# Per-expert tile counts read one expert ahead, and a later place for the next expert's first transposes, in a fused attention and mixture-of-experts kernel

## The chip, the cores and the metric

The kernel runs on one core of a Trainium2 chip. The metric is device microseconds of one execution; the number given for the kernel before is the median of three runs. Beside these runs there is one profiled execution, and every duration below comes from it.

## The reference

The reference chains three blocks on 4608 tokens of width 512. The first is attention over keys and values that are mean-pooled by eight. The second sends each token that passes a skip score through one of eight experts, the third is a dense layer with a SoLU and a layer norm. Only the second one matters for the change:

```python
    do_compute = skip_score > 0
    ...
    e_idx = np.argmax(logits, axis=1)
    ...
    for e in range(E):
        mask = e_idx == e
        if not mask.any():
            continue
        h = np.maximum(xc[mask] @ w1[e], 0.0)
        y[mask] = gate_w[mask, None] * (h @ w2[e])
    out[do_compute] = xc + y
```

How many tokens an expert gets is known only at run time.

## The kernel before

The kernel is one instruction stream per engine, in the order in which the Python code is written. It has three stages: attention with routing (about 0 to 228 us), the experts (228 to 620 us) and the dense layer (620 us to the end).

**Routing** scatters each token's index and gate weight into a table, sorted by expert, in HBM. At the end of the attention stage the token counts of the eight experts are turned, on VectorE (DVE), into a small integer tile `nti` in SBUF (lines 785 to 793). A count is in half tiles of 64 tokens, at least 2. `nti` holds four groups of eight: the count, its half (whole tiles of 128), its odd bit, and the half limited to the last table column.

**The expert stage** is a Python loop over e (line 1084). Tokens of one expert are worked off in tiles of 128 by `body(e, q_, work)` (line 965): a gather of the token rows (`gather`, an indirect DMA issued by GpSimd, POOL), four transposes on TensorE (PE) into the one PSUM tile `pxt` with a scaled copy to f16 on ScalarE (ACT, line 922) and the rounding rest on DVE (line 923) (`trans`), four groups of matmuls with the first weight (`mm1_group`, line 938, 24 matmuls a group) each followed by the ReLU on ACT (line 942) and its rounding rest on DVE (line 943), the matmuls with the second weight in two halves (`mm2`, line 950), and `fin`: gate and residual on DVE (line 954) and a scatter by POOL (line 955). Every operand is held as an f16 high part and an f16 rest.

**What lies between the groups** is handed to `body` as a list `work`, one entry after each group, one between the halves of `mm2`, what is left at the end. For the first tile of an expert the list holds the preparation of expert e+1: eight weight pieces (`wnext`, piece i: `w_split` makes the high part on ACT, line 114, and the rest on DVE, line 119; for piece 4 on POOL, lines 116 and 117; then the load of piece i of expert e+2 is queued) and the transposes of the first tile of expert e+1. In the kernel before these transposes are third in the list for every expert, so they stand behind group 2 (counted from 0) and before group 3.

**Half tiles.** An expert with an odd count has one tile of 64 rows more. Its rows' addresses and gates are copied by DVE into `hidx` and `hgat` from a table column that is known only at run time (lines 1010 and 1011), its rows are gathered at the start of the expert (line 1012), and `half(e)` runs under `tc.If(odd[e] > 0)` (line 1114) between the first and the second tile. Its ReLU rest is line 1037, its second matmul line 1041. The second and later tiles stand in nested Ifs on the count (line 1129).

**Counts into registers.** Behind the first tile of expert 0 every engine reads eight counts and eight odd bits from `nti` into registers, and DVE eight column numbers besides (lines 1100 to 1104). An If that isn't taken still keeps order: an engine whose next work needs buffers that the If's body might have used waits until the others have passed it.

In this input expert 0 has an even count (three tiles), experts 1 and 7 are even, expert 4 has one tile, and experts 2, 3, 5 and 6 have a half tile.

Of the kernel before, what the change touches and what calls it, by code (L numbers as in the profile page):

```python
# [10 lines left out]
I32 = mybir.dt.int32  # L11
AF = mybir.ActivationFunctionType
ALU = mybir.AluOpType
# [28 lines left out]
def fused_kernel(  # L42
# [15 lines left out]
    nc = tc.nc  # L58
    V, S, G, T = nc.vector, nc.scalar, nc.gpsimd, nc.tensor
    B, H, SEQ, D = q.shape  # L60
    NTOK, DM = out.shape
    E, _, DF = w1.shape
    NT = NTOK // P
# [9 lines left out]
    cp = ctx.enter_context(tc.tile_pool(name="cp", bufs=1))  # L73
# [47 lines left out]

    tabv = cp.tile([P, NT, 2], F32, name="tabv")
    row = cp.tile([P, NT], I32, name="row")
    nti = cp.tile([1, 4 * E], I32, name="nti")
    tbe = cp.tile([P, E * NT, 2], F32, name="tbe")
    tbs = []
    idx0 = cp.tile([P, 1], I32, name="idx0")
# [2 lines left out]
    with ExitStack() as actx:  # L130
# [653 lines left out]
        cnt = ac.tile([P, E], F32, name="cnt")  # L784
        V.tensor_tensor(cnt, base[rt["n"] % 2][:, 0:E], base0[:, 0:E], ALU.subtract)
        cni = ac.tile([P, E], I32, name="cni")

        V.tensor_scalar(cni, cnt, 63.0, None, ALU.add)
        V.tensor_scalar(cni, cni, 6, None, ALU.logical_shift_right)
        V.tensor_scalar(nti[:, 0:E], cni[0:1, :], 2.0, None, ALU.max)  # L790
        V.tensor_scalar(nti[:, E:2 * E], nti[:, 0:E], 1, None, ALU.logical_shift_right)
        V.tensor_scalar(nti[:, 2 * E:3 * E], nti[:, 0:E], 1, None, ALU.bitwise_and)
        V.tensor_scalar(nti[:, 3 * E:], nti[:, E:2 * E], NT - 1.0, None, ALU.min)
        for i in range(4, 7):
            w_split(0, i)

# [11 lines left out]
    def d_load(i, eng=nc.sync):  # L808
        a = w_in if i < 4 else w_out
        if wide:  # L810
            a = a.bitcast(I32)
        st_ = dst[i % 2]
        if i < 4:
            eng.dma_start(st_, a[i * P:(i + 1) * P, :])
        else:
            j = 2 * (i - 4)
            eng.dma_start(st_.rearrange("p (c d) -> p c d", c=2),
                              a[j * P:(j + 2) * P, :].rearrange("(c p) d -> p c d", p=P))
# [44 lines left out]
    def m_load(i):  # L863
        t_ = xg[gset(E, i)] if i < NPRE else fp.tile([P, DM], F32, tag="x2", name="x2", bufs=3)
        (G if i < NPRE else nc.sync).dma_start(t_, m_rows(xres[P:XROWS, :], i))
        sx[i] = {"x": t_}
# [11 lines left out]
    with ExitStack() as mctx:  # L878
# [5 lines left out]
        tbi = mp_.tile([P, E * NT + 1], I32, name="tbi")  # L884
        tb = tbe
# [16 lines left out]
        hidx = [mp_.tile([P, 1], I32, name=f"hidx{i}") for i in range(2)]  # L902
        hgat = [mp_.tile([P, 1], F32, name=f"hgat{i}") for i in range(2)]

        def gset(e, q_):
            return q_ % 3 if q_ > 2 else 4 + 2 * q_ + e % 2 if q_ else 3 + e % 3

        def tset(e, q_):
                return q_ % 2 if q_ else 2 + e % 2
# [5 lines left out]
        def trans(g_, s_, pe=False, w=P):  # L915
            h_, l_ = xt[s_][:, 0:NKC, 0:w], xt[s_][:, NKC:, 0:w]
            if pe:
                for kc in range(NKC):
                    T.transpose(pxt[:, kc * P:kc * P + w], xg[g_][0:w, kc * P:(kc + 1) * P],
                                ident[0:w, 0:w])  # L920
                px = pxt.rearrange("p (c t) -> p c t", c=NKC)[:, :, 0:w]
                S.activation(h_, px, AF.Copy, scale=SX1)
                V.scalar_tensor_tensor(l_, px, SX1, h_, ALU.mult, ALU.subtract)
                return
            hl = xhl[s_ // 2]
            S.activation(hl[:, 0:DM], xg[g_], AF.Copy, scale=SX1)
            V.scalar_tensor_tensor(hl[:, DM:], xg[g_], SX1, hl[:, 0:DM], ALU.mult, ALU.subtract)
            nc.sync.dma_start_transpose(xt[s_], hl)
# [36 lines left out]
        def body(e, q_, work):  # L965

            c = e * NT + q_
            s_, hb = tset(e, q_), q_ % 2
            if q_ + 2 < nstatic and (q_ or e == 0):
                gather(gset(e, q_ + 2), idx_of(c + 2))  # L970
            if q_ == 0 and e:
                half_rows(e)
            if q_ == 0 and e + 1 < E:
                for j, r in ((e + 2, 0), (e + 1, 1), (e + 1, 2)):
                    if j < E:
                        gather(gset(j, r), idx_of(j * NT + r))

            first = e == 0 and q_ == 0
            pe = q_ < 2
            if q_ + 1 < nstatic and not pe:  # L980
                trans(gset(e, q_ + 1), tset(e, q_ + 1))
            work = list(work)

            def step(n=1):
                for _ in range(n):
                    if work:
                        work.pop(0)()

            for gq in range(4):
                mm1_group(e, s_, hb, gq, q_)  # L990
                if gq == 1 and pe and not first:
                    trans(gset(e, q_ + 1), tset(e, q_ + 1), True)
                step()
            mm2(e, hb, 0, 4)
            if first:
                trans(gset(e, q_ + 1), tset(e, q_ + 1), True)
            elif q_ == 0:
                half_trans()
            step(1)
            mm2(e, hb, 4, 8)  # L1000
            step(len(work))
            fin(gset(e, q_), hb, gate_of(c), idx_of(c))

        HG, HT = 1, 0

        def half_rows(e):
            o_ = hq[e] + e * NT
            V.tensor_scalar(hidx[e % 2], tbi[:, bass.ds(o_, 1)], 0.0, None, ALU.add)  # L1010
            V.tensor_scalar(hgat[e % 2], tb[:, bass.ds(o_, 1), 1], 0.0, None, ALU.add)
            G.indirect_dma_start(out=xg[HG][0:64], out_offset=None, in_=xbuf,
                                 in_offset=bass.IndirectOffsetOnAxis(ap=hidx[e % 2][0:64], axis=0))

# [59 lines left out]
        def wnext(e, i):  # L1074

            w_split(e + 1, i, i == 4)
            if e == 0 and i < 4:
                w_load(e + 1, i + 4, nc.scalar)
            if e + 2 < E:
                w_load(e + 2, i)  # L1080
# [3 lines left out]
        for e in range(E):  # L1084


            last = e + 1 == E
            works = {q_: [] for q_ in range(nstatic)}
            if not last:
                sp = [lambda e=e, i=i: wnext(e, i) for i in range(8)]  # L1090
                works[0] += sp[0:2] + [lambda e=e: trans(gset(e + 1, 0), tset(e + 1, 0), True)] + sp[2:6]
                works[1] += sp[6:]
            if e < 2:
                works[1].append(lambda e=e: d_load(e))
            for n, j in enumerate(DP.get(e, ())):
                works[n if last else n + 1] += [lambda f_=f_, j=j: f_(j)
                                                for f_ in (d_decode, d_split, d_next)]
            body(e, 0, works[0])
            if e == 0:
                cnts = [nc.values_load(nti[0:1, j:j + 1], min_val=2, max_val=2 * NT) for j in range(E)]  # L1100
                hq = [nc.values_load(nti[0:1, 3 * E + j:3 * E + j + 1],
                                     engines=[mybir.EngineType.DVE], min_val=0, max_val=NT - 1) for j in range(E)]
                odd = [nc.values_load(nti[0:1, 2 * E + j:2 * E + j + 1], min_val=0, max_val=1)
                       for j in range(E)]
            if last:
                m_load(0)
                works[1].append(lambda: m_xt(0))
                for i in range(1, NPRE):
                    works[min(i + 1, nstatic - 1)] += (
                        [lambda i=i: m_load(i)] + 3 * [lambda: None] + [lambda i=i: m_xt(i)])  # L1110

            with tc.If(odd[e] > 0):  # L1114
                if e == 0:
                    half_rows(e)
                    half_trans()
                half(e)

            def rest(q_):  # L1120

                if q_ == nstatic:
                    with tc.If(cnts[e] > 2 * q_ + 1):  # L1123
                        n = nc.values_load(nti[0:1, E + e:E + e + 1], min_val=0, max_val=NT)
                        with tc.For_i(nstatic, n, 1, name=f"rest{e}") as j:
                            loop_tile(e, j)
                    return
                todo = [f_ for r in range(q_, nstatic) for f_ in works[r]]
                with tc.If(cnts[e] > 2 * q_ + 1) as full:  # L1129
                    body(e, q_, works[q_])  # L1130
                    rest(q_ + 1)
                if todo:
                    with full.Else():
                        for f_ in todo:
                            f_()

            rest(1)
# [140 lines left out]
```

## Time and profile before

| what | us |
|---|---|
| median of three runs (lowest, highest) | 1006.11 (1002.54, 1011.88) |
| the profiled execution | 1002.64 |
| its span, first to last instruction | 1000.9 |
| PE busy in the span | 889.9 |

The profiled execution is near the lowest of the three runs and 3.47 us below their median; 1.74 us of it lie outside the span. In the rows, times are microseconds from the span's start: start, busy time, engine, line and operation, result and operands, how often, and in brackets the idle time of the engine before it with what ended it. "DVEq L1114" means that the engine was released when DVE's instruction queue passed line 1114. "PEld" is PE's weight load.

### The profile page before, as it was taken

To read this page: it belongs to the slowest core of one execution; us is meant where nothing else is said; L and a number is where in the kernel's file an instruction comes from. 1 tells how busy PE (TensorE), PEld (TensorE's weight loads), DVE (VectorE), ACT (ScalarE), POOL (GpSimd) and SP (SyncE) were. 2 spreads that over 40 slices of the span, in tenths; PEclk is the share of its full clock that TensorE was granted. 3 is DMA by queue.
4 is the path that set the end of the run, shared out by engine and by line. 5 is a ranking of instruction groups with operands and counts; after the bars stand their busy time and mean duration, and the time that the engine had idled before them with its cause. 6 is when DMAs were issued, how large, how long until landed. Compare 5 with 4: busy or idle time off the path is not lost. (4 is left out here: it accounts for less than half of the span.)

```text
span 1000.9 us, 20355 instructions
## 1 busy us (share of the span) xinstructions
PE 889.9 (89%) x7838; PEld 565.3 (56%) x7838; DVE 628.3 (63%) x1419; ACT 430.4 (43%) x1002; POOL 299.3 (30%) x255
## 2 busy tenths in 40 slices
PE   5898899855497888689898999989999999999998
PEld 4687777645375566566676676434444444444443
DVE  7599888996344554665564732666666666666652
ACT  3476667733223343432432321445445344443432
POOL 3692967675213433452331220000000000000000
PEclk9698989987798999899999999999999999999999
DMA  9799867366547555765162641457756656657443
GB/s 284 234 322 330 281 225 253 123 222 191 174 148 241 173 179 160 237 187 178 50 164 80 150 85 55 92 112 135 153 130 138 138 125 124 140 110 149 100 91 88
DMA packets 189310, 163.99 MB, mean 164 GB/s; under 512 B 137296, under 2 KB 145488, under 8 KB 188656
## 3 DMA queue, kind: packets, MB, share of 16 engines
q1 hardware_dynamic: 180880, 140.50, 52.4%
q0 software_dynamic: 7200, 19.57, 6.2%
q10 hardware_dynamic: 1088, 2.10, 0.6%
q8 instruction: 80, 1.31, 0.6%
q14 instruction: 62, 0.51, 0.2%
HBM read 94.95 MB, written 38.01 MB: 133 GB/s over the span
## 5 line engine op out<-in xcount | busy, mean ns | idle before, releaser
L1215 PE MATMUL po<-woh,zt 128*128 128x512 f16 x576 | 176.7, 379 | 3.1 <-ACT o L1218 2.0
L1152 PE MATMUL ph<-wih,xt 128*128 128x512 f16 x576 | 176.7, 379 | 1.0 <-DVEq L1123 1.0
L1215 PEld LDWEIGHTS <-zt 128*128 128x128 f16 x864 | 84.4, 98 | 105.7 <-issue 2.3
L1152 PEld LDWEIGHTS <-xt 128*128 128x128 f16 x864 | 84.4, 98 | 103.2 <-issue 1.5
L1191 POOL TENSOR_TENSOR rr<-va,mhalf 128x1 f32<-128x1 f32 x36 | 19.8, 549 | 342.9 <-DVE va L1190 342.9
L1174 ACT ACTIVATE wst<-ph,ng 128x512 f32<-128x512 f32 x72 | 48.8, 682 | 158.2 <-DVE ng L1170 146.0
L942 ACT ACTIVATE hh<-ph 128x256 f16<-128x256 f32 x104 | 39.0, 380 | 172.5 <-PE ph L938 164.3
L1152 PE MATMUL ph<-wil,xt 128*128 128x512 f16 x288 | 109.2, 379 | 0.0
L1215 PE MATMUL po<-wol,zt 128*128 128x512 f16 x288 | 109.2, 379 | 0.0
L938 PE MATMUL ph<-xt,wsb 128*128 128x128 f16 x1536 | 95.4, 225 | 13.7 <-PEq L1129 9.2
L938 PEld LDWEIGHTS <-wsb 128*128 128x128 f16 x1536 | 92.6, 101 | 19.2 <-issue 16.5
L943 DVE SCALAR_TENSOR_TENSOR hl<-ph,hh 128x256 f16<-128x256 f32 x104 | 43.0, 421 | 60.8 <-ACT hh L942 59.1
L938 PE MATMUL ph<-xt,wsa 128*128 128x128 f16 x960 | 60.7, 225 | 22.3 <-DVEq L1114 13.7
L950 PE MATMUL py<-wsb,hh 128*128 128x512 f16 x256 | 76.2, 379 | 0.0
L938 PEld LDWEIGHTS <-wsa 128*128 128x128 f16 x960 | 58.4, 102 | 26.3 <-DVEq L1114 14.2
L1206 DVE SCALAR_TENSOR_TENSOR zl<-wst,zh 128x1024 f16<-128x1024 f32 x36 | 44.1, 1225 | 45.3 <-ACT zh L1204 45.3
L955 POOL DMA_INDIRECT xres<-yo,tbi x26 | 28.8, 1109 | 140.0 <-DVE yo L954 77.2
L1178 DVE SCALAR_TENSOR_TENSOR wst<-ph,wst 128x512 f32<-128x512 f32 x72 | 49.0, 692 | 30.5 <-ACT wst L1174 30.5
L505 PE MATMUL px<-vbh,ah 128*128 128x148 f16 (+1 forms) x320 | 52.7, 231 | 15.4 <-DVE lraw L538 11.6
L269 POOL TENSOR_TENSOR kv<-kv 128x1280 f32<-128x1280 f32 (+3 forms) x28 | 57.1, 2041 | 22.2 <-DMA kv<-in_k_dram 21.0
L1157 DVE TENSOR_REDUCE mx<-ph 128x1 f32<-128x512 f32 x72 | 49.4, 686 | 21.1 <-PE ph L1152 21.1
L950 PEld LDWEIGHTS <-hh 128*128 128x128 f16 x416 | 39.0, 98 | 41.1
(384 smaller groups left out, 1841.0 us busy)
## 6 DMA issues: line engine op xcount, KB each, us to landing
wst<-in_moe_w_dram SPq DMA_DIRECT2D x60, 512.0 KB, 4.7
out_dram<-o SPq DMA_DIRECT2D x36, 256.0 KB, 2.4
x<-xres SPq DMA_DIRECT2D x33, 256.0 KB, 3.3
kv<-in_v_dram SPq DMA_DIRECT2D x8, 1024.0 KB, 9.7
xbuf<-xs SPq DMA_DIRECT2D x16, 512.0 KB, 3.5
xres<-xs SPq DMA_DIRECT2D x16, 512.0 KB, 7.8
kv<-in_k_dram SPq DMA_DIRECT2D x7, 1024.0 KB, 8.8
qm<-in_q_dram SPq DMA_DIRECT2D x7, 1024.0 KB, 9.1
```

Source lines behind the costliest of these rows:

```text
L269: eng.tensor_tensor(x_[:, :, 0:r, :], x_[:, :, 0:r, :], x_[:, :, r:2 * r, :], ALU.add)
L505: T.matmul(hd[sl, a, h:h + x1 - x0, :], s_, w_[rw, c0 + x0:c0 + x1, :], start=(n == 0 and bl == 2 * a), stop=(n == 2 and bl == 2 * a + 2))
L938: T.matmul(o_, ww[:, kc * DF + fc * P:kc * DF + (fc + 1) * P], xt[s_][:, x0 + kc, :], start=(n == 0), stop=(n == 11))
L942: S.activation(hh[hb][:, sl], ph, AF.Relu)
L943: V.scalar_tensor_tensor(hl[hb][:, sl], ph, 0.0, hh[hb][:, sl], ALU.max, ALU.subtract)
L950: T.matmul(py[hb], xx[:, fc * P:(fc + 1) * P], ww[:, fc * DM:(fc + 1) * DM], start=(fc == 0 and n == 0), stop=(fc == NFC - 1 and n == 2))
L1152: T.matmul(ph, xt[:, xx, :], ww[:, ws], start=(n == 0), stop=(n == 11))
L1157: V.tensor_reduce(sx[i]["mx"][:, half:half + 1], ph, axis=AX.X, op=ALU.max)
L1174: S.activation(e_[:, o_], ph[a], AF.Exp, bias=ng, scale=CE, accum_out=s2[:, a:a + 1])
L1178: V.scalar_tensor_tensor(u_[:, o_], ph[a], 1.0, e_[:, o_], ALU.mult, ALU.mult, accum_out=su[:, a:a + 1])
L1206: V.scalar_tensor_tensor(zl, u_, SZ, zh, ALU.mult, ALU.subtract)
L1215: T.matmul(po, zt[:, xx, :], ww[:, ws], start=(fc == 0 and n == 0), stop=(fc == NFC - 1 and n == 2))
```

## The change

It has three parts.

1. `nti` keeps two groups instead of four: whole tiles, and the count. Counts at or above 72 half tiles are brought to 70, so that a shift by one gives a legal column.
2. The registers are no longer read in one block. A new function `half_cols(e)` reads one count into a register on every engine, works the table column out of it (shift and add) and lets DVE fill `hidx` and `hgat`. It is called for expert 0 and expert 1 behind the first tile of expert 0, then for expert e+1 behind the first tile of expert e. `half_rows` keeps the gather alone. The If on the odd bit now computes `count & 1` in a register.
3. In expert 0 the transposes of expert 1's first tile go to the end of the list (behind `mm2`); in the other experts they move back by one place, behind group 3, and weight piece 2 moves forward by one.

```diff
--- before.py
+++ after.py
@@ -121,7 +121,7 @@
 
     tabv = cp.tile([P, NT, 2], F32, name="tabv")
     row = cp.tile([P, NT], I32, name="row")
-    nti = cp.tile([1, 4 * E], I32, name="nti")
+    nti = cp.tile([1, 2 * E], I32, name="nti")
     tbe = cp.tile([P, E * NT, 2], F32, name="tbe")
     tbs = []
     idx0 = cp.tile([P, 1], I32, name="idx0")
@@ -785,12 +785,12 @@
         V.tensor_tensor(cnt, base[rt["n"] % 2][:, 0:E], base0[:, 0:E], ALU.subtract)
         cni = ac.tile([P, E], I32, name="cni")
 
+
         V.tensor_scalar(cni, cnt, 63.0, None, ALU.add)
         V.tensor_scalar(cni, cni, 6, None, ALU.logical_shift_right)
-        V.tensor_scalar(nti[:, 0:E], cni[0:1, :], 2.0, None, ALU.max)
-        V.tensor_scalar(nti[:, E:2 * E], nti[:, 0:E], 1, None, ALU.logical_shift_right)
-        V.tensor_scalar(nti[:, 2 * E:3 * E], nti[:, 0:E], 1, None, ALU.bitwise_and)
-        V.tensor_scalar(nti[:, 3 * E:], nti[:, E:2 * E], NT - 1.0, None, ALU.min)
+        V.tensor_scalar(nti[:, E:], cni[0:1, :], 1, None, ALU.logical_shift_right)
+        V.tensor_scalar(cnt, cni, 2.0 * NT, -2.0, ALU.is_ge, ALU.mult)
+        V.scalar_tensor_tensor(nti[:, 0:E], cni[0:1, :], 2.0, cnt[0:1, :], ALU.max, ALU.add)
         for i in range(4, 7):
             w_split(0, i)
 
@@ -1004,11 +1004,17 @@
 
 
         HG, HT = 1, 0
-
-        def half_rows(e):
-            o_ = hq[e] + e * NT
+        cnts = {}
+
+        def half_cols(e):
+
+            cnts[e] = nc.values_load(nti[0:1, e:e + 1], min_val=2, max_val=2 * NT - 1)
+            o_ = nc.s_assert_within((cnts[e] >> 1) + e * NT, e * NT + 1, (e + 1) * NT - 1,
+                                    skip_runtime_bounds_check_because="71 >> 1 is 35")
             V.tensor_scalar(hidx[e % 2], tbi[:, bass.ds(o_, 1)], 0.0, None, ALU.add)
             V.tensor_scalar(hgat[e % 2], tb[:, bass.ds(o_, 1), 1], 0.0, None, ALU.add)
+
+        def half_rows(e):
             G.indirect_dma_start(out=xg[HG][0:64], out_offset=None, in_=xbuf,
                                  in_offset=bass.IndirectOffsetOnAxis(ap=hidx[e % 2][0:64], axis=0))
 
@@ -1088,7 +1094,9 @@
             works = {q_: [] for q_ in range(nstatic)}
             if not last:
                 sp = [lambda e=e, i=i: wnext(e, i) for i in range(8)]
-                works[0] += sp[0:2] + [lambda e=e: trans(gset(e + 1, 0), tset(e + 1, 0), True)] + sp[2:6]
+                nx = lambda e=e: trans(gset(e + 1, 0), tset(e + 1, 0), True)
+
+                works[0] += sp[0:3] + [nx] + sp[3:6] if e else sp[0:6] + [nx]
                 works[1] += sp[6:]
             if e < 2:
                 works[1].append(lambda e=e: d_load(e))
@@ -1097,11 +1105,9 @@
                                                 for f_ in (d_decode, d_split, d_next)]
             body(e, 0, works[0])
             if e == 0:
-                cnts = [nc.values_load(nti[0:1, j:j + 1], min_val=2, max_val=2 * NT) for j in range(E)]
-                hq = [nc.values_load(nti[0:1, 3 * E + j:3 * E + j + 1],
-                                     engines=[mybir.EngineType.DVE], min_val=0, max_val=NT - 1) for j in range(E)]
-                odd = [nc.values_load(nti[0:1, 2 * E + j:2 * E + j + 1], min_val=0, max_val=1)
-                       for j in range(E)]
+                half_cols(0)
+            if not last:
+                half_cols(e + 1)
             if last:
                 m_load(0)
                 works[1].append(lambda: m_xt(0))
@@ -1111,7 +1117,7 @@
 
 
 
-            with tc.If(odd[e] > 0):
+            with tc.If((cnts[e] & 1) > 0):
                 if e == 0:
                     half_rows(e)
                     half_trans()
```

In the order of instructions this gives two changes on DVE and one on PE. The first is DVE in the first tile of expert 0, from the second ReLU rest on. `hl` is the ReLU rest, `wsb` the rest of expert 1's weight pieces (from staging tiles `wst_77` to `wst_81`, pieces 1, 2, 3 and 5), `xt_4359` and `xt_4360` of before are the transposed second tile of expert 0 and first tile of expert 1. Before:

```order
L943 SCALAR_TENSOR_TENSOR hl_4363<-ph_4370,hh_4361 128x256
L923 SCALAR_TENSOR_TENSOR xt_4360<-pxt,xt_4360 128x512
L943 SCALAR_TENSOR_TENSOR hl_4363<-ph_4371,hh_4361 128x256
L119 SCALAR_TENSOR_TENSOR wsb_4321<-wst_78,wsb_4320 128x1024
L923 SCALAR_TENSOR_TENSOR xt_4359<-pxt,xt_4359 128x512
L119 SCALAR_TENSOR_TENSOR wsb_4321<-wst_79,wsb_4320 128x1024
L119 SCALAR_TENSOR_TENSOR wsb_4323<-wst_81,wsb_4322 128x1024
L954 SCALAR_TENSOR_TENSOR yo_4365<-py_4373,tbe,xg_99 128x512
```

Of the change, the same place (every buffer number is one lower; `xt_4359` is now expert 1's first tile):

```order
L943 SCALAR_TENSOR_TENSOR hl_4362<-ph_4369,hh_4360 128x256
L119 SCALAR_TENSOR_TENSOR wsb_4320<-wst_78,wsb_4319 128x1024
L943 SCALAR_TENSOR_TENSOR hl_4362<-ph_4370,hh_4360 128x256
L119 SCALAR_TENSOR_TENSOR wsb_4320<-wst_79,wsb_4319 128x1024
L923 SCALAR_TENSOR_TENSOR xt_4358<-pxt,xt_4358 128x512
L119 SCALAR_TENSOR_TENSOR wsb_4322<-wst_81,wsb_4321 128x1024
L923 SCALAR_TENSOR_TENSOR xt_4359<-pxt,xt_4359 128x512
L954 SCALAR_TENSOR_TENSOR yo_4364<-py_4372,tbe,xg_99 128x512
```

The transposes of expert 1's first tile have gone from between the third and fourth ReLU rest to the place right before `fin`, and weight piece 2 stands one ReLU rest earlier.

The second is DVE from the end of the first tile of expert 0 to the If of line 1114. Before, 24 register loads stand there (eight of each kind; the ISA rows are checks of the column numbers, and seven more pairs of a load and its checks are left out):

```order
L954 SCALAR_TENSOR_TENSOR yo_4365<-py_4373,tbe,xg_99 128x512
L1100 TENSOR_LOAD nti x8
L1101 TENSOR_LOAD nti
L1101 ISA x2
...
L1103 TENSOR_LOAD nti x8
L1114 COMPARE_AND_BRANCH
```

Of the change, all that stands there (line 1011 is the load, 1014 and 1015 the two column copies, 1120 the If):

```order
L954 SCALAR_TENSOR_TENSOR yo_4364<-py_4372,tbe,xg_99 128x512
L1011 TENSOR_LOAD nti
L1014 ISA
L1014 TENSOR_SCALAR hidx_4376<-tbi 128x1
L1015 ISA
L1015 TENSOR_SCALAR hgat_4378<-tbe 128x1
L1011 TENSOR_LOAD nti
L1014 ISA
L1014 TENSOR_SCALAR hidx_4377<-tbi 128x1
L1015 ISA
L1015 TENSOR_SCALAR hgat_4379<-tbe 128x1
L1120 REGISTER_ALU
```

24 loads have become two, and four column copies, two of which stood in the If and two at the start of expert 1, have moved to this place.

The third is DVE at the same point of a later expert (here expert 1), where before the If followed `fin` at once. Of the change:

```order
L954 SCALAR_TENSOR_TENSOR yo_4364<-py_4372,tbe,xg_4349 128x512
L1011 TENSOR_LOAD nti
L1014 ISA
L1014 TENSOR_SCALAR hidx_4376<-tbi 128x1
L1015 ISA
L1015 TENSOR_SCALAR hgat_4378<-tbe 128x1
L1120 REGISTER_ALU
L1120 COMPARE_AND_BRANCH
L1043 SCALAR_TENSOR_TENSOR hh_4361<-ph_4371,hh_4361 128x4x64
```

A load, two column copies and a register operation now stand between `fin` and the half tile's ReLU rest (line 1043, line 1037 of before); PE, ACT, POOL and SP have the load and the register operation at the same point.

## Rows read from the trace of the kernel before

**Rows 1.** Busy time by engine, of the page:

```profile
PE 889.9 (89%) x7838; PEld 565.3 (56%) x7838; DVE 628.3 (63%) x1419; ACT 430.4 (43%) x1002; POOL 299.3 (30%) x255
```

**Rows 2.** Windows: stretch, length, then busy time of PE, PEld, DVE, ACT, POOL, clock:

```profile
254.82:268.48 13.66, 0.00 (x1) 0.00 (x1) 3.08 (x3) 0.88 (x1) 6.95 (x4) 0.66 0.54 181
...
620.00:1000.90 380.90, 373.62 (x1728) 168.82 (x1728) 232.48 (x611) 166.03 (x321) 20.71 (x37) 1.00 0.57 121
```

**Rows 3.** Timeline of PE, first two tiles of expert 0:

```profile
232.55 4.46 PE L938 MATMUL ph<-xt,wsa 128*128 128x128 f16 x72 [0.81 <-ACT xt L922]
245.60 1.12 PE L919 MATMUL pxt<-ident,xg 128*128 128x128 f32 x4 [8.59 <-DMA xg<-xbuf,tbi]
246.51 2.69 PE L938 MATMUL ph<-xt,wsa 128*128 128x128 f16 x24
249.04 0.59 PE L950 MATMUL py<-wsa,hh 128*128 128x512 f16 x2
...
268.48 4.94 PE L938 MATMUL ph<-xt,wsa 128*128 128x128 f16 x48 [13.66 <-DVEq L1114]
```

**Rows 4.** Timeline of DVE, ACT and POOL, first tile of expert 0:

```profile
244.88 0.42 DVE L943 SCALAR_TENSOR_TENSOR hl<-ph,hh 128x256 f16<-128x256 f32 x1
...
252.90 0.69 DVE L923 SCALAR_TENSOR_TENSOR xt<-pxt,xt 128x512 f16<-128x512 f32 x1 [1.07 <-ACT xt L922]
255.73 2.17 DVE L119 SCALAR_TENSOR_TENSOR wsb<-wst,wsb 128x1024 f16<-128x1024 f32 x1 [0.67 <-ACT wsb L114]
257.82 0.74 DVE L954 SCALAR_TENSOR_TENSOR yo<-py,tbe,xg 128x512 f32<-128x512 f32 x1
...
252.27 0.60 ACT L922 ACTIVATE xt<-pxt 128x512 f16<-128x512 f32 x1 [1.70 <-PE pxt L919]
252.76 2.94 ACT L114 ACTIVATE wsb<-wst 128x1024 f16<-128x1024 f32 x3
...
241.77 1.04 POOL L912 DMA_INDIRECT xg<-xbuf,tbi  x1 [0.30 <-issue]
260.04 1.02 POOL L955 DMA_INDIRECT xres<-yo,tbi  x1 [0.16 <-issue]
267.37 0.97 POOL L912 DMA_INDIRECT xg<-xbuf,tbi  x1 [6.30 <-DMA xg<-xbuf,tbi]
```

**Rows 5.** Timeline of DVE, start of expert 4:

```profile
395.54 0.15 DVE L1010 TENSOR_SCALAR hidx<-tbi 128x1 int32 x1 [0.55 <-DVEq L1129]
395.69 0.15 DVE L1011 TENSOR_SCALAR hgat<-tbe 128x1 f32 x1
```

**Rows 6.** Timeline of DVE and PE, half tile of expert 3:

```profile
378.47 0.74 DVE L954 SCALAR_TENSOR_TENSOR yo<-py,tbe,xg 128x512 f32<-128x512 f32 x1
379.13 0.74 DVE L1037 SCALAR_TENSOR_TENSOR hh<-ph,hh 128x256 f16<-128x256 f32 x2
379.59 2.76 PE L1041 MATMUL py<-wsb,hh 128*128 128x512 f16 x12 [1.01 <-DVE hh L1037]
```

**Rows 7.** Waits of PE, 292 to 560 us: total us, times, longest:

```profile
PE pxt L919 <- issue: 5.6, 3, 2.0
PE ph L938 <- DVEq L1114: 4.4, 2, 3.5
PE py L1041 <- DVE hh L1037: 4.0, 4, 1.0
...
PE pxt L919 <- DMA xg<-xbuf,hidx: 2.9, 1, 2.9
PE pxt L919 <- DVE xt L923: 2.5, 5, 0.6
```

**Rows 8.** Timeline of PE: matmuls behind waits, experts 1, 4 and 5:

```profile
311.29 5.28 PE L938 MATMUL ph<-xt,wsb 128*128 128x128 f16 x48 [3.53 <-DVEq L1114]
...
396.50 2.85 PE L938 MATMUL ph<-xt,wsa 128*128 128x128 f16 x48 [2.29 <-PEq L1129]
...
417.21 5.07 PE L938 MATMUL ph<-xt,wsb 128*128 128x128 f16 x46 [6.15 <-PEq L1129]
```

## The prediction

> **What bounds the kernel now.** I read the page first, then the windows by stage, then PE's idle time in the timeline of the expert stage, and last DVE, ACT and POOL beside each gap. PE is busy for 889.9 us of a span of 1000.9 [rows 1]. In the dense stage it works 373.62 of 380.90 us [rows 2]; the change touches nothing there, so that stage only moves in time. The gaps lie among the experts, and the two longest stand at the first tile of expert 0 [rows 3]. PE stops after three groups of matmuls at 237.01 (232.55 + 4.46) and waits 8.59 us for the gather of expert 1's first tile, whose transposes stand third in its list. At 254.82 it is through with the tile and waits 13.66 us more, until 268.48: no matmul falls in that stretch [rows 2, 3].
>
> What ends the second gap is named: DVE's queue passing line 1114. DVE finished `fin` at 258.56 (257.82 + 0.74) [rows 4], so from there to 268.48 it took 9.92 us to do nothing but the 24 register loads, their checks and the branch. That makes at most 0.41 us a load. POOL gives the same from another side: 16 loads and its own waits fill the 6.30 us before its next gather, at most 0.39 us each [rows 4].
>
> **Part 1: the loads behind the first tile.** Two loads are left on DVE (0.82 at 0.41 each), and with each come two column copies of 0.15 us, which start 0.15 us apart [rows 5]; with some 0.2 us for the register operation and the branch that is 0.82 + 0.60 + 0.2 = 1.6 us in place of 9.92. Saved: 8.3 us. If nothing is hidden and each copy first pays the 0.55 us that DVE sat idle before line 1010 [rows 5], it is 0.82 + 0.60 + 4 x 0.55 = 3.6 us (6.3 saved); if the second load hides under the copies, 1.1 (8.8 saved). The fewer operations that make `nti` lie in routing and are worth under 0.2 us; I count nothing. PE, ACT and POOL have two loads instead of 16 as well, and wait for DVE either way.
>
> **Part 2: the transposes behind the first tile.** Group 3 no longer waits for expert 1's rows. Its 24 matmuls follow at the pace of the 72 before them (62 ns each), 1.5 us, and end at 238.5. What bounds the tile next is DVE. It is held by the table of indices until its first ReLU rest, and the third one still ends at 245.30 (244.88 + 0.42): the rows up to there don't change [rows 4]. Then, in the new order: piece 2 (1.2, as its sisters take), fourth ReLU rest (0.4), piece 3 (1.2), rest of the second tile's transposes (0.7), piece 5 (2.17, as now, while POOL does piece 4), rest of expert 1's transposes (0.7), `fin` (0.74). The sum is 7.1 us: `fin` ends at 252.4 if no other engine is late. PE isn't: the 24 second matmuls and four transposes that ran from 249.04 to 254.82 (5.78 us) [rows 3] start as the ReLU rests come and end near 248 to 250. ACT has to do the second tile's copy (0.60), two weight pieces (2 of the 3 that took 2.94) and the new last copy (0.60) [rows 4] behind PE's transposes, and is done near 250.5. I allow 0.6 us for these handovers: `fin` ends at 253.0 instead of 258.56, and 5.5 us are saved. From both sides: 6.2 if DVE runs without a hole, 4 if PE's clock falls in its wait for the ReLU rests. [...] The ACT queue starts two weight loads some 11 us sooner, beside the gathers of 240 to 248; a gather that lands 1 to 2 us later is inside the 0.6 and the 4.
>
> Behind this PE still waits (about 250 to 254.6), so its first matmuls of the second tile run slowly as they do now (48 in 4.94 us [rows 3]); no change.
>
> **Part 3: what the later experts pay.** Experts 1 to 6 now read the next count behind their first tile. The place matters on DVE. In a half tile (experts 2, 3, 5, 6) line 1037 starts 0.66 us after `fin` starts, back to back, and PE waits 1.01 us for it [rows 6], four times 4.0 us in all [rows 7]. A load and two copies now stand between. In expert 1 PE waits 3.53 us for DVE to pass the If [rows 8], which comes later by as much. The cost is 0.30 for the copies if the load runs while `fin` does, as the branch evidently does now; 0.41 + 0.30 + 0.1 = 0.8 if it doesn't; 1.4 with the 0.55 us before a copy on top. I take 0.55, between the first two, in five experts: 2.75 us (1.5 to 7.0). PE's own load lies in the same waits. Expert 4 has neither a half nor a second tile: there the load meets PE's 6.15 us of waiting [rows 8] on a chain I can't split, and I add one load, 0.4 (0 to 1.2). Expert 7 reads nothing. What leaves the start of an expert, lines 1010 and 1011, was in DVE's idle time and gives nothing.
>
> [...] The 0.41 us above come from a row of loads and can't show what one alone costs. [...]
>
> The moved transposes spare PE its wait for the single `pxt` before them, 2.5 us in five experts [rows 7]. Those five are experts 1, 2, 3, 4 and 6. But in 1, 3 and 4 PE waits again a little later, before the half tile's transposes, whose gather POOL times (the row "issue" is this wait in experts 1, 4 and 5, up to 2.0 us [rows 7]); what is spared there is waited there. Only experts 2 and 6 keep it: 0.55 us each, 1.1 us (0 to 2.5).
>
> **Sum.** -8.3 - 5.5 + 2.75 + 0.4 - 1.1 = -11.75 us. On the profiled execution that is 1002.64 - 11.75 = 990.9; its 3.47 us below the median are kept, so the median would be 1006.11 - 11.75 = 994.4 us. With the bounds of the terms added the cautious way, the own range is about -8 to -15.
>
> **Rivals.**
> - *The transposes give nothing.* What sets `fin` might be something the new order doesn't free: the weight pieces, with POOL's piece 4 making DVE's piece 5 slow, or a gather that lands late behind the earlier weight loads. For it: piece 5 takes 2.17 us and ends only at 257.90 now [rows 4]. Against it: ACT, which releases it, is itself late only because PE's transposes were (1.70 us idle). Then -8.3 + 3.15 - 1.1 = -6.25, 999.9 us.
> - *A lone load is dear.* The load waits for DVE to be empty and nothing hides it: 1.4 us in five experts and 1.2 in expert 4, 8.2 in place of 3.15. For it: 0.55 us of idle time before the copy now [rows 5]. Against it: the branch in that place costs nothing now [rows 6]. Then -13.8 - 1.1 + 8.2 = -6.7, 999.4 us.
> [...]
>
> **How the numbers follow.** The forecast has 0.66, the two lesser gains 0.17 and 0.14, the slower case 0.03. About 1% (10 us) is what a measurement of this kernel can tell from no change. Of the forecast, a fifth falls short of 10 us (its terms at their weak ends, or the scatter of the runs): 0.53 faster and 0.13 within. The two lesser gains fall within 1% except for 0.01. So faster 0.54, within 0.43, slower 0.03. The range goes from 988 (-18: all terms at their good ends and the runs nearer to their lowest) to 1003 (-3: a lesser gain with the scatter of the runs, which reached from 1002.54 to 1011.88).
>
> **What would show each step right or wrong.** In the profile after: no wait of PE for a gather of expert 1 within the first tile; the fourth group of line 938 right behind the third; `fin` of that tile ending near 253 and PE starting the second tile 1 to 3.6 us behind it, near 254.6; the wait of PE for line 1037's successor (1043) near 1.5 us in experts 2, 3, 5 and 6, and at most 2.4; 48 matmuls behind it as fast as now. The forecast is wrong if DVE needs more than 4 us from `fin` to the second tile, if `fin` ends behind 256, or if the waits in the half tiles grow by over 1.5 us each.

## The result, and the profile after

| | median us (lowest, highest) | runs |
|---|---|---|
| before, beside the changed kernel | 1007.54 (1002.54, 1011.88) | 4 |
| after | 992.64 (989.22, 993.73) | 4 |
| after over before | 0.9855, interval 0.9817 to 0.9893 | |

The change saves 14.9 us, 1.5%. The forecast was 994.4 us with a range of 988 to 1003. The profiled execution of the changed kernel took 993.73 us. Every ratio, here and below, leaves out executions more than 1.5% above the fastest of the same kernel, which the medians keep, so a ratio isn't the quotient of two medians.

The first view to read is the windows by stage. Each row is a stretch, its length, PE's busy time and count, the granted clock, DMA share and rate. The stages are attention with routing, the experts, and the dense layer; the second begins at PE's first matmul of line 938. The kernel before:

```profile
0.00:232.55 232.55, 189.40 (x2426) 0.87 0.78 249
232.55:620.30 387.75, 326.90 (x3684) 0.96 0.52 154
620.30:1000.90 380.60, 373.62 (x1728) 1.00 0.57 121
```

After:

```profile
0.00:237.78 237.78, 199.04 (x2426) 0.89 0.73 244
237.78:611.44 373.66, 333.13 (x3685) 0.95 0.54 160
611.44:992.00 380.56, 373.62 (x1728) 1.00 0.57 121
```

The expert stage is 14.09 us shorter and the dense stage the same to 0.04 us. The attention stage came out 5.23 us longer in this execution. Little of it is touched, and its length changes with the execution: in the profiles below the expert stage begins between 229.56 and 237.78 us, whichever kernel it is. So two profiles are compared from the first matmul of line 938 on, never from the start of the span, and every place of after stands 5.23 us further than it would beside the trace of before. PE is busy 333.13 us in the expert stage against 326.90 with the same work, so its idle time there fell from 60.85 to 40.53 us. Matmuls that took 6.2 us longer gave some of that back; whether they are the change's doing is taken up below.

PE in the first tile of expert 0, where [rows 3] showed the two long waits:

```profile
237.78 5.80 PE L938 MATMUL ph<-xt,wsa 128*128 128x128 f16 x96 [0.81 <-ACT xt L922]
...
247.64 0.61 PE L950 MATMUL py<-wsa,hl 128*128 128x512 f16 x1 [3.63 <-DVE hl L943]
...
254.19 0.60 PE L919 MATMUL pxt<-ident,xg 128*128 128x128 f32 x4
258.57 5.30 PE L938 MATMUL ph<-xt,wsa 128*128 128x128 f16 x48 [3.78 <-DVEq L1120]
```

All 96 matmuls of the four groups run in one piece: the wait for expert 1's gather is gone. Expert 1's transposes are the last thing in the tile (254.19), and the wait behind them is 3.78 us instead of 13.66. From the first matmul to the second tile it is 20.79 us (258.57 - 237.78) against 35.93 (268.48 - 232.55 [rows 3]).

DVE in the same place, for [rows 4]:

```profile
254.32 2.63 DVE L119 SCALAR_TENSOR_TENSOR wsb<-wst,wsb 128x1024 f16<-128x1024 f32 x1 [0.60 <-ACT wsb L114]
256.88 0.68 DVE L923 SCALAR_TENSOR_TENSOR xt<-pxt,xt 128x512 f16<-128x512 f32 x1
257.48 0.73 DVE L954 SCALAR_TENSOR_TENSOR yo<-py,tbe,xg 128x512 f32<-128x512 f32 x1
258.13 0.14 DVE L1014 TENSOR_SCALAR hidx<-tbi 128x1 int32 x1
258.19 0.14 DVE L1015 TENSOR_SCALAR hgat<-tbe 128x1 f32 x1
258.25 0.14 DVE L1014 TENSOR_SCALAR hidx<-tbi 128x1 int32 x1
258.31 0.14 DVE L1015 TENSOR_SCALAR hgat<-tbe 128x1 f32 x1
```

`fin` ends at 258.21 (257.48 + 0.73), and the four copies follow it 0.06 us apart with no hole. Two register loads stand among them in the order of instructions and can't be seen here. PE starts 0.36 us after `fin`.

The half tile of expert 3, for [rows 6]:

```profile
368.55 0.74 DVE L954 SCALAR_TENSOR_TENSOR yo<-py,tbe,xg 128x512 f32<-128x512 f32 x1
369.21 0.14 DVE L1014 TENSOR_SCALAR hidx<-tbi 128x1 int32 x1
369.27 0.14 DVE L1015 TENSOR_SCALAR hgat<-tbe 128x1 f32 x1
369.33 0.74 DVE L1043 SCALAR_TENSOR_TENSOR hh<-ph,hh 128x256 f16<-128x256 f32 x2
...
369.80 3.63 PE L1047 MATMUL py<-wsb,hh 128*128 128x512 f16 x16 [1.13 <-DVE hh L1043]
```

The load is hidden here too. Only the two copies stand between, and PE waits 1.13 us where it waited 1.01.

Waits of PE in experts 1 to 6 and the start of expert 7 (279 to 548 us; total, times, longest), for [rows 7]:

```profile
PE ph L938 <- PEq L1135: 11.5, 7, 4.8
PE pxt L919 <- issue: 8.0, 3, 4.0
PE py L1047 <- DVE hh L1043: 3.4, 3, 1.1
PE ph L938 <- DVEq L1120: 3.1, 2, 2.2
```

The wait for the single `pxt` (line 923, 2.5 us in five) is gone, and the wait before a half tile's transposes ("issue") has grown from 5.6 to 8.0. The half tiles' wait for line 1043 stands there three times instead of four: in expert 5 PE comes late, behind 3.96 us of "issue", and finds the ReLU rests done.

### The profile page after: what moved, and what is told of

Its sections match the earlier page's. It is cut to its first block, busy times and chain, and to the rows that moved or that the text cites. A ratio compares the mean times of both kernels' runs of the same rounds, so it can differ in the third digit from the quotient of the medians.

```text
span 992.0 us, 20314 instructions
## 1 busy us (share of the span) xinstructions
PE 905.8 (91%) x7838; PEld 575.1 (58%) x7838; DVE 627.4 (63%) x1420; ACT 430.7 (43%) x1002; POOL 299.4 (30%) x255
## 5 line engine op out<-in xcount | busy, mean ns | idle before, releaser
L938 PE MATMUL ph<-xt,wsb 128*128 128x128 f16 x1536 | 95.2, 225 | 11.5 <-PEq L1135 8.3
L950 PE MATMUL py<-wsb,hh 128*128 128x512 f16 x256 | 79.1, 392 | 0.0
```

The source lines that it names most:

```text
L938: T.matmul(o_, ww[:, kc * DF + fc * P:kc * DF + (fc + 1) * P], xt[s_][:, x0 + kc, :], start=(n == 0), stop=(n == 11))
L950: T.matmul(py[hb], xx[:, fc * P:(fc + 1) * P], ww[:, fc * DM:(fc + 1) * DM], start=(fc == 0 and n == 0), stop=(fc == NFC - 1 and n == 2))
```

## The experiments

Medians are of the timed runs of a kernel, ratios to the kernel before on the same chip with their 95% intervals. "First stretch" is the time from PE's first matmul of line 938 to its second tile, in the profiled execution: 35.93 us before, 20.79 after.

| kernel | median us | ratio (interval) | first stretch us |
|---|---|---|---|
| loads alone | 994.79 | 0.9883 (0.9804 to 0.9962) | 25.89 |
| transposes alone, expert 0 | 999.56 | 0.9942 (0.9902 to 0.9983) | 30.56 |
| the change, later experts in the old order | 992.11 | 0.9835 (0.9767 to 0.9903) | 20.60 |
| before with 16 loads | 1001.73 | 0.9960 (0.9934 to 0.9985) | 30.90 |
| the change with four loads an expert | 991.34 | 0.9791 (0.9752 to 0.9830) | 20.65 |
| the change again | 994.27 | 0.9868 (0.9840 to 0.9895) | 20.50 |
| the change, third time | 990.61 | 0.9853 (0.9804 to 0.9903) | 20.93 |
| piece 5 in the second tile | 985.40 | 0.9815 (0.9741 to 0.9890) | 19.67 |
| the same again | 986.90 | 0.9810 (0.9758 to 0.9862) | 19.90 |
| pieces 4 and 5 in the second tile | 1006.71 | 1.0007 (0.9971 to 1.0043) | 23.51 |

### One part at a time

**Loads alone**: the changed kernel with the transposes in the old place in every expert.

```diff
-                works[0] += sp[0:3] + [nx] + sp[3:6] if e else sp[0:6] + [nx]
+                works[0] += sp[0:2] + [nx] + sp[2:6]
```

> The change without the move: the transposes of the next expert's first tile stay third in the list in every expert. Theory (the two parts add, each with its own gap): fin of the first tile ends as late as before (21.0 us behind the second group's first matmul of that expert... in the profile before 258.56 - 232.55 = 26.0 us behind PE's first matmul of the expert), and the second tile starts 0.4 us behind fin instead of 9.9: about 9.5 us saved there, 0.12 us lost in each of four half tiles, ratio to before near 0.991. Rival (the two parts are worth something only together, because another engine with its own loads or copies ends late when the loads are gone): the second tile starts over 3 us behind fin, ratio above 0.995.

PE waits 7.98 us for the gather again, and the second wait is short:

```profile
242.00 1.12 PE L919 MATMUL pxt<-ident,xg 128*128 128x128 f32 x4 [7.98 <-DMA xg<-xbuf,tbi]
...
254.36 0.74 DVE L954 SCALAR_TENSOR_TENSOR yo<-py,tbe,xg 128x512 f32<-128x512 f32 x1
...
255.45 1.81 PE L938 MATMUL ph<-xt,wsa 128*128 128x128 f16 x19 [4.10 <-DVEq L1120]
```

The first stretch is 25.89 us, so the loads by themselves save 10.04 there. `fin` ends at 255.10, 0.35 us before PE starts.

**Transposes alone**: the kernel before, with the transposes moved in expert 0.

```diff
-                works[0] += sp[0:2] + [lambda e=e: trans(gset(e + 1, 0), tset(e + 1, 0), True)] + sp[2:6]
+                nx = lambda e=e: trans(gset(e + 1, 0), tset(e + 1, 0), True)
+                works[0] += sp[0:2] + [nx] + sp[2:6] if e else sp[0:6] + [nx]
```

> The kernel before with the transposes moved in expert 0 alone, 24 loads kept. Theory: PE's wait for the gather of expert 1's tile goes, fin of the first tile ends about 20.4 us behind PE's first matmul of the expert (as in the change) instead of 26.0, the 9.9 us of loads stand behind it as before: about 5.6 us saved, ratio near 0.994. Rival (the loads overlap more when fin comes sooner, or the move is hidden under the loads): the second tile starts no earlier than before, ratio 0.999 to 1.001.

```profile
233.27 5.80 PE L938 MATMUL ph<-xt,wsa 128*128 128x128 f16 x96 [0.81 <-ACT xt L922]
...
252.81 0.74 DVE L954 SCALAR_TENSOR_TENSOR yo<-py,tbe,xg 128x512 f32<-128x512 f32 x1
...
263.83 2.42 PE L938 MATMUL ph<-xt,wsa 128*128 128x128 f16 x21 [13.64 <-DVEq L1115]
```

The first stretch is 30.56 us, 5.37 less. `fin` ends at 253.55 (DVE starts it at 252.81 for 0.74), 20.28 us behind the first matmul, and the 24 loads then hold PE until 263.83: 10.28 us. The two parts make 10.04 + 5.37 = 15.41 us, together they saved 15.14. In this stretch they add: no part hides behind the other, since both stand on one chain, DVE to the If. The whole expert stage of one profile is too coarse to show it: the profiled execution of the transposes alone was the slowest of its ten (1006.37 us), and its expert stage took 390.61 us, longer than the 387.75 before, in spite of the 5.37 us saved at its start.

**The later experts in the old order**: the change, with its new place for the transposes in expert 0 alone.

```diff
-                works[0] += sp[0:3] + [nx] + sp[3:6] if e else sp[0:6] + [nx]
+                works[0] += sp[0:2] + [nx] + sp[2:6] if e else sp[0:6] + [nx]
```

> The change, but experts 1 to 6 keep the old third place of the transposes. Theory: the wait for pxt before them returns in experts 1, 2, 3, 4 and 6 (about 0.5 us each, 2.5 us together), but about half of it is taken back from the wait before the half tile's transposes; the time is 1 to 1.5 us above the change, ratio to before near 0.987. Rival (nothing is saved in experts 1 to 6): the same as the change within 0.5 us, with the waits for the half tile's gather shorter by what the wait for pxt adds.

The waits for `pxt` are back (2.1 us in four), the wait before the half tiles' transposes is 7.9 us as in the change (8.0), and the time can't be told from it. The move by one place in the later experts is worth nothing that these times can show.

### What a load costs

**Sixteen loads**: the kernel before, with the column number worked out from the count in a register, as the change does it, but all loads still in a row behind expert 0's first tile.

```diff
...
-            o_ = hq[e] + e * NT
+            o_ = nc.s_assert_within((cnts[e] >> 1) + e * NT, e * NT + 1, (e + 1) * NT - 1,
...
-                hq = [nc.values_load(nti[0:1, 3 * E + j:3 * E + j + 1],
-                                     engines=[mybir.EngineType.DVE], min_val=0, max_val=NT - 1) for j in range(E)]
```

> The kernel before, but DVE's eight loads of column numbers and their checks are left out (the column is worked out of the count register, as in the change): 16 loads behind the first tile in place of 24, the counts capped one lower. Theory (a load costs 0.4 to 0.45 us of DVE's sequencer, and what is queued ahead of it hides about the first two): from the end of fin to the second tile 5.5 to 6.6 us instead of 9.9, ratio near 0.9965. Rival (the eight column loads with their checks were the cost): under 3 us, ratio near 0.993.

```profile
256.22 0.74 DVE L954 SCALAR_TENSOR_TENSOR yo<-py,tbe,xg 128x512 f32<-128x512 f32 x1
...
261.86 3.34 PE L938 MATMUL ph<-xt,wsa 128*128 128x128 f16 x34 [8.65 <-DVEq L1113]
```

From `fin`'s end (256.96) to the second tile it is 4.90 us, less than expected. The eight column loads with their two checks each were 5.02 of the 9.92 us before, 0.63 us each. The other 16 loads show 0.31 each. So 0.41 us was not the price of every load: either the column loads are the dear ones, or a part of the row lies beside earlier work, or both.

**Four loads**: the change, where experts 1 to 6 read the next count four times instead of once.

```diff
-            cnts[e] = nc.values_load(nti[0:1, e:e + 1], min_val=2, max_val=2 * NT - 1)
+            ld = [nc.values_load(nti[0:1, e:e + 1], min_val=2, max_val=2 * NT - 1)
+                  for _ in range(4 if e > 1 else 1)]
+            cnts[e] = ld[0]
+            for l_ in ld[1:]:
+                cnts[e] = cnts[e] & l_
```

> The change, but experts 1 to 6 read the next count four times and join the four by three register operations before each use. Theory (the sequencer of DVE runs ahead: fin and the copies are queued behind weight piece 5, so the loads run beside it and cost nothing there): PE's wait before the half tile's second matmul stays between 1.1 and 1.5 us in experts 2, 3 and 6, time within 2 us of the change. Rival (a load in that place is paid in full, and the 0.12 us seen in the change is one load half hidden): four loads of 0.4 us make the wait 2.2 to 2.9 us, 5 to 8 us in all.

DVE and PE at the half tile of expert 2 (lines 1018, 1019 and 1047 are the copies and the ReLU rest):

```profile
336.17 2.17 DVE L119 SCALAR_TENSOR_TENSOR wsb<-wst,wsb 128x1024 f16<-128x1024 f32 x1 [0.67 <-ACT wsb L114]
338.26 0.74 DVE L954 SCALAR_TENSOR_TENSOR yo<-py,tbe,xg 128x512 f32<-128x512 f32 x1
338.92 0.14 DVE L1018 TENSOR_SCALAR hidx<-tbi 128x1 int32 x1
338.98 0.14 DVE L1019 TENSOR_SCALAR hgat<-tbe 128x1 f32 x1
339.20 0.76 DVE L1047 SCALAR_TENSOR_TENSOR hh<-ph,hh 128x256 f16<-128x256 f32 x2
...
339.68 3.63 PE L1051 MATMUL py<-wsa,hh 128*128 128x512 f16 x16 [1.30 <-DVE hh L1047]
```

Three more loads bring PE's wait from 1.13 to 1.30 us here, to 1.35 and 1.33 us in experts 3 and 6, and to 0.21 in expert 5, where PE comes late. The first copy still follows `fin` at once (0.66 us from start to start); what is added stands between the second copy and the ReLU rest, 0.22 us from start to start instead of 0.06. The copies need the loaded number, so the loads were made while DVE worked on piece 5 and `fin`: DVE's sequencer took them ahead of its queued work. How far ahead it can take them, no run here shows.

**Piece 5 in the second tile**: the change, with weight piece 5 in the work of the second tile instead of the first. DVE then has only the rest of expert 1's transposes queued before `fin`.

```diff
-                works[0] += sp[0:3] + [nx] + sp[3:6] if e else sp[0:6] + [nx]
-                works[1] += sp[6:]
+                works[0] += sp[0:3] + [nx] + sp[3:5] if e else sp[0:5] + [nx]
+                works[1] += sp[5:]
```

> The change with weight piece 5 moved from the end of the first tile to the list of the second tile, in every expert. Theory (in the change fin and all behind it on DVE wait for piece 5, 2.2 to 2.6 us on DVE while POOL works on piece 4): fin of expert 0's first tile ends 2 to 2.6 us sooner, the 1.13 us before the half tiles' second matmul go in four experts, expert 1's 2.24 us before its second tile go at least in part: 6 to 9 us below the change, ratio to before near 0.978. Rival (piece 5 then delays the second tile's own DVE work or PE waits for ACT instead): no more than 2 us below the change.

```profile
249.51 0.69 DVE L923 SCALAR_TENSOR_TENSOR xt<-pxt,xt 128x512 f16<-128x512 f32 x1 [2.08 <-ACT xt L922]
250.12 0.74 DVE L954 SCALAR_TENSOR_TENSOR yo<-py,tbe,xg 128x512 f32<-128x512 f32 x1
250.78 0.14 DVE L1014 TENSOR_SCALAR hidx<-tbi 128x1 int32 x1
250.96 0.15 DVE L1015 TENSOR_SCALAR hgat<-tbe 128x1 f32 x1
251.52 0.15 DVE L1014 TENSOR_SCALAR hidx<-tbi 128x1 int32 x1 [0.40 <-issue]
251.72 0.15 DVE L1015 TENSOR_SCALAR hgat<-tbe 128x1 f32 x1
```

The second load comes into view: DVE had waited 2.08 us for ACT, little was queued, and 0.40 us of idle time stand before the third copy, 0.56 us from one copy's start to the next. PE starts at 252.15, 1.29 us after `fin` ended, near the 1.6 of the prediction and not the 0.36 of the change. So the price of a load is there; the change pays it under DVE's queue. The first stretch got only 1.1 us shorter, where the moved piece had taken over 2, since 0.9 of it went to the loads that came into view.

### A version that may beat the change, and one that doesn't

**Piece 5 again, beside the change.** The kernel with piece 5 moved had been some 7 us under the change, in separate comparisons.

> The kernel with the shared piece of sp[5] in the second tile, timed again side by side with the change. If the 7 us that it had been under the change in separate jobs are its own, it comes to 985 to 990 us here and the change beside it to 992 to 995. If they were scatter of the attention stage, both come within 3 us of each other.

> The change itself, beside the kernel with the piece moved: 992 to 995 us, 0.985 to 0.989 of the kernel before.

On one chip they came to 986.90 (980.35 to 995.91) and 990.61 (985.58 to 992.65), six runs each, with ratios of 0.9810 (0.9758 to 0.9862) and 0.9853 (0.9804 to 0.9903). Moving the piece was ahead both times, here by 3.7 us, but the intervals overlap. About 1 us of the gain is seen in the first stretch (19.67 and 19.90 against 20.50 to 20.93); how much of the rest is its own stays open. The expert stage was 370.17 and 376.40 us in the two profiles with the piece moved, 373.66, 376.98 and 373.78 in three of the change, so the profiles don't tell them apart either. The change itself was timed three times: 992.64, 994.27, 990.61.

> The change itself once more, beside the version above on the same chip. Both theories: 12 to 17 us below the kernel before, fin to second tile under 0.6 us, wait before the half tiles' second matmul 1.13 us.

**Pieces 4 and 5 in the second tile** (the same edit with `sp[0:4]` and `sp[4:]`).

> The change with weight pieces 4 and 5 both in the second tile's list. Theory (fin of the first tile then waits for no weight piece, POOL is free for its scatter, and the second tile has room for both): the waits before the half tiles' second matmul go, expert 1's wait before its second tile falls below 1.2 us, time 5 to 9 us below the change. Rival (POOL's piece 4, 5 us long, now holds back the second tile's scatter and with it the next expert's gathers): PE's waits for the half tile's gather grow by 1 us or more each, and the time is that of the change or above it.

The whole gain is lost, though not by a gather. PE waits 27.5 us in seven waits before an expert's first matmuls where it waited 11.5 (13.9 and 14.4 in the other two profiles of the change, 18.4 and 18.1 with piece 5 alone moved). It also waits for a ReLU rest in two tiles, up to 3.1 us. The waits of PE from 272 to 548 us:

```profile
PE ph L938 <- PEq L1135: 27.5, 7, 5.9
PE ph L938 <- DVE hl L943: 6.3, 2, 3.1
```

I suspected the branch that does an expert's remaining pieces when it has no second tile: it is jumped over in seven experts and grows with each piece. Two kernels leave it out except in expert 4, which alone needs it for this input:

```diff
-                if todo:
+                if todo and (e == 4 or q_ > 1):
```

> The change without the Else that does an expert's remaining weight pieces when it has no second tile, except in expert 4, the one expert that has none here. That branch is jumped over in every other expert. If the jump over it makes PE wait behind each expert's second tile (11.5 us in seven waits for PE's queue in the change), these waits fall to under 6 us and the time by about 4 to 6 us, to 987 to 989. If the waits come from the weight pieces themselves or from the scatter, they stay at 11 to 14 us and the time at 991 to 994.

> Pieces 4 and 5 in the second tile, again without that Else outside expert 4. If the jump over a longer branch is what gave the gain back (27.5 us in seven waits instead of 11.5), these waits fall below 10 us and the time to 985 to 990. If piece 4 on POOL itself, or the late weights, hold the next expert back, the waits stay above 20 us and the time at 1002 to 1007.

They took 991.19 us (0.9882, 0.9806 to 0.9959) and 1011.93 us (1.0059, 1.0014 to 1.0103). The waits stayed, 13.6 us in the first and in the second (the waits of PE from 272 to 560 us):

```profile
PE ph L938 <- PEq L1135: 27.1, 7, 5.6
```

So the jump over this branch isn't it. What PE waits for there after pieces 4 and 5 have been moved is open. Piece 4 on POOL doesn't hold back the scatter (line 955) that stands behind it. At the end of expert 2, with both pieces moved:

```profile
346.97 1.01 POOL L955 DMA_INDIRECT xres<-yo,tbi  x1 [3.58 <-POOLq L1135]
...
351.44 4.85 PE L938 MATMUL ph<-xt,wsb 128*128 128x128 f16 x48 [5.54 <-PEq L1135]
```

POOL had been idle for 3.58 us and started the scatter 0.28 us after `fin` (346.69), yet PE starts 4.47 us behind it; in the change PE started 0.58 us behind the scatter there (351.56, 352.14). The waits in front of experts 6 and 7 are 0.58 us in both kernels. The experts before those two have four tiles, experts 0 to 4 at most three, so what comes after the pieces within an expert may matter: its remaining tiles, or the Ifs on tiles that it doesn't have. No run took these apart.

## Why the prediction was right

The forecast of 994.4 us was 1.8 us above the measured 992.64, and the gain, 11.75 by the sum, was 14.09 in the expert stage of the traces and 14.9 in the medians. That the time came so close is in part luck: the median of the kernel before was 1006.11 for the forecast and 1007.54 beside the result, and from that one the sum would have given 995.8. Both ways of saving time were as argued. Term by term:

- **Transposes behind the tile, -5.5: right.** `fin` of the first tile was to end at 253.0; it ended at 258.21, which is 252.98 beside the trace of before. Alone the move saved 5.37. DVE sets it, as argued: it works from 254.32 to the end of `fin` without a hole, behind 0.60 us of waiting for ACT. PE's clock did fall in the wait for the ReLU rests (3.63 us; the granted clock is 0.91 from 244.10 to 247.64 and 0.59 from there to 251.00, and two matmuls of `mm2` take 1.06 us instead of 0.59), but PE is done at 254.79 and DVE 3.42 us later. Through ACT the slow matmuls can have cost at most the 0.60 us that DVE waited. No run shows the 4 us put down for a falling clock: it fell here, and `fin` came 5.58 us sooner (258.56 - 252.98). That the sum met `fin` to 0.02 us is luck: piece 5 took 2.63 us instead of 2.17, and against that DVE's instructions started 0.07 to 0.09 us before the one ahead had ended.
- **Loads, -8.3: mis-sized; it was -9.56** (9.92 - 0.36). The step that failed is the 0.82 us for two loads at "at most 0.41 us a load", paid behind `fin`. The loads took nothing there, and the four copies 0.24 us (to 258.45) in place of 0.60. The price counted the loads from the end of `fin`, as if none could begin earlier, and so gave the row's mean as a bound on what a load adds. In a row of 24 a little hidden at the front can't be seen; with two, all of it is hidden. The lower end of the prediction, 1.1 us from `fin` to the second tile, still kept one load in view.
- **Later experts, +2.75: mis-sized; the half tiles pay 0.12 us each** (1.13 - 1.01, in three of four; with the loads alone in all four, 4.5 us together), and expert 1 waited less at its If than before (2.24 against 3.53 [rows 8]; 1.17 and 2.40 in the other two profiles of the change). With the old order in the later experts that wait was 3.65 us twice, so it may have shrunk by the new order and not by the loads; the kernel with 16 loads, in the old order too, had 1.97. The prediction set 0.30 for two copies with the load hidden as its good end, and chose 0.55. Even that end was too dear: copies start 0.06 us apart behind queued work, where [rows 5] shows 0.15 on an idle engine. The 0.4 us for expert 4 isn't seen: the wait behind it is 4.77 us instead of 6.15 (5.86 and 5.89 in the other two profiles).
- **Experts 2 and 6, -1.1: not seen.** The wait for `pxt` went, and the waits before the half tiles grew from 5.6 to 8.0 us; with the old order in the later experts the time was the same. The other two profiles of the change have 11.7 and 8.9 us there, so a gain of 1 us can't be read from these waits.
- **The rest.** From expert 0's second tile on, the expert stage lost 1.05 us in the traces (15.14 gained, 14.09 kept); the sum had 2.05 for that. One profile can't confirm it: the change's other two lost 4.66 and 1.03 us there. Nor are the matmuls, 6.2 us longer in this stage, shown to be the change's doing. PE is busy 331.94 us there with the transposes alone and 331.29 with 16 loads, and both keep the order of before in the later experts; it is the 326.90 of before that stands apart.

The rival "the transposes give nothing" falls with 5.37 us measured. "A lone load is dear" falls twice: 0.12 us in place of 1.4, and four loads still cost no more than 0.22 (1.35 - 1.13). With it falls the slower case, which had a chance of 0.03: no half tile of the change waited over 1.13 us for its ReLU rest, and the 16 second matmuls of expert 2's half tile and the 48 behind them run as fast as before (3.63 and 2.84 us). Elsewhere, though, 48 matmuls behind short waits did run slower in this profile, in two of these three places:

```profile
301.73 4.40 PE L938 MATMUL ph<-xt,wsb 128*128 128x128 f16 x48 [2.24 <-DVEq L1120]
...
352.14 4.48 PE L938 MATMUL ph<-xt,wsb 128*128 128x128 f16 x48 [2.39 <-PEq L1135]
...
385.75 2.85 PE L938 MATMUL ph<-xt,wsa 128*128 128x128 f16 x48 [1.34 <-PEq L1135]
```

The windows of these three stretches give granted clocks of 0.62, 0.62 and 1.00. In the kernel before it is 1.00 behind the 2.29 us of [rows 8] and 0.50 behind the 3.53, but the length of the wait alone sets no border between the two: with the loads alone, the tile of 352.14 starts at 352.00 behind 2.40 us and its 48 matmuls take 2.85. Nor is it the change that slows them. With the transposes alone, whose later experts are those of before, expert 3 starts so, in 4.48 us behind 2.02:

```profile
361.77 4.48 PE L938 MATMUL ph<-xt,wsb 128*128 128x128 f16 x48 [2.02 <-PEq L1130]
```

## What to carry to other kernels

A register load on an engine with work queued ahead of it cost next to nothing here (three more added at most 0.22 us together). Rows of 16 and 24 loads showed 4.90 and 9.92 us behind `fin`, and with little queued ahead, after 2.08 us of waiting, 0.56 us passed from one copy's start to the next with a load between them. So a block of loads belongs spread out, one behind each stretch of long instructions, and not in a row where several engines meet at an If. When a price is read from a row of equal instructions, ask first what part of the row may have begun before the row's visible start: the mean is then neither a bound nor the cost of one.

## What the runs showed of the hardware that was not expected

- Two 128x1 copies on DVE start 0.06 us apart behind a queued instruction (258.13, 258.19), but 0.15 us apart on an idle engine [rows 5].
- The first 48 matmuls of expert 3 took 4.48 us behind a wait of 2.39 us in the change, at a granted clock of 0.62, and 2.85 us behind one of 2.40 us with the loads alone. The wait alone doesn't decide.
- The start of the expert stage moved over 8.2 us among the profiles (229.56 to 237.78), with code in front of it that is the same but for a few small instructions, and over 4.6 us among three of the same kernel (233.16 to 237.78). It goes into a run's time as it is, and is a part of the scatter of up to 17 us between runs of one kernel.
